# Attention backward on one core: dK/dV products of both key chunks in one step, and transposes in column tiles of 32

## The chip, the core and the metric

The kernel runs on one core of a Trainium2 chip. The core has a matrix engine (TensorE, PE in the profile; its weight loads are listed apart as PEld), a vector engine (VectorE, DVE), an activation engine (ScalarE, ACT), GpSimd (POOL) and SyncE (SP), which here issues most of the DMAs. The metric is the device time of one execution in microseconds (us). The kernel before took 2742.68 us, the median of 3 runs (2736.2 to 2745.76).

## What is computed

The reference takes the gradient of a block `x + attention(ln(x)) * silu(mlp(ln(ln(x))))` with respect to x and to all weights. Sequence length is 2048, model width 512, 32 heads of 16. What matters here is the attention with its backward pass. Cut to that part, the reference is

```
xn = layernorm(x);  qkv = xn @ wqkv
scores = einsum("bhqd,bhkd->bhqk", q, k) * (Dh ** -0.5)
p = softmax(scores);  o = einsum("bhqk,bhkd->bhqd", p, v);  s = o @ wo
out = x + s * g          # g = silu(mlp(xn))
# and jax.vjp of all this: d(x), d(wqkv), d(wo), d(w1), d(b1), d(w2), d(b2)
```

For each head the backward needs E = exp(scores), the products D = V dO^T, and G = E * D elementwise; then dQ from G K, and dK and dV from G^T Q, E^T Q and E^T dO, with the softmax's row sums folded into small weights.

## The kernel before

Three parts run one after the other: a part ahead (`phase_pre`: layer norms, projections, the MLP), the attention (`attention_core`), and the weight gradients (`phase3`). The change is in the attention alone. In the profile its first score product starts 285.7 us after the span's start and its last Z product ends at 2135.1 us, so it takes 1849 of the 2738 us.

**Blocks and steps.** Heads go in 16 pairs. For a pair, the 2048 queries are cut into 4 chunks of 512; pair and query chunk make a block, of which there are 64. A block goes over the 2048 keys in 16 key blocks of 128. One key block of one block is a *step* `g`: 1024 steps, `g % 16` is the place in the block. Four key blocks make a key chunk `kc`, and two key chunks a pair `kp`. The order of the instructions on each engine is written by hand: the loop at L841 emits, for each `g`, the calls at L853 to L869 in that order, and nothing reorders them (`manual_schedule`).

**What a step does.** On TensorE, in this order:

- `emit_z` (L786): Z products of an older block, 21 steps behind (`ZG`, `ZE`, L835). They are dK and dV for one key chunk and one quarter `qb` of the queries. Part 1 multiplies the transposed G (`Gk`) by the weights `W2`, part 0 the transposed E (`Ek`) by `W1`, each for two heads `hj`. An output is 32 rows of the accumulator Z at row `64*par + 32*hj`, `par = kc % 2`. `ZORD` (L605) alternates the even and the odd key chunk from step to step.
- `emit_s` and `emit_d` (L629, L647): s = K Q^T of the next step and d = V dO^T of this step, two heads each. Contraction is over 32 rows, and the four products sit in the four row groups of the array. Together they are called the score phase here.
- `emit_T` (L686, L694): in three steps of four (not where `g % 4 == 3`), the transpose of one quarter of the queries' E for the key chunk before: 8 transposes of 128x128 into one PSUM tile `tT`. The fourth quarter is transposed by a DMA (L678), and so is G (L674).
- `emit_x` (L707): X products of the step before, 6 of them with 32 (or 17) output rows each: `l` at rows 64 and 96, `e` at rows 0 and 32, `g` at rows 64 and 96.

ScalarE takes the exponentials of both s tiles (L635, `et`), and then copies `tT` to SBUF (L704, `ek`). VectorE multiplies d and E (L660, `gts`). Once per block, at step 2 (`FIN_AT`), TensorE transposes X (L744), and VectorE and GpSimd make from it the block's outputs and the weights W1 and W2 (`emit_fin`, L747). After every eight Z steps VectorE adds Z to `acc` (L821, steps 4 and 12).

**What sets who waits.** PSUM has three buffers for s and tT together (`ps_st`), three for d and the X transpose (`ps_d`), and one each for X and Z. A score product waits until ScalarE has read the buffer that it writes, a transpose group waits for the buffer of an earlier one, a d product waits for VectorE's multiply of an earlier d, and the first Z product of a key chunk pair waits until VectorE has read Z.

Of the kernel before, what the change touches and what calls it, by code (L numbers as in the profile page):

```python
# [9 lines left out]
f32 = mybir.dt.float32  # L10
# [532 lines left out]
def attention_core(ctx, tc, NAT_s, NATQ_s, Oall, dQall, dKVT_out, ident_f32, ident_bf, npairs=16, nqc=4):  # L543
    nc = tc.nc
# [5 lines left out]
    ps_z = ctx.enter_context(tc.tile_pool(name="ps_z", bufs=1, space=PSUM))  # L550
# [24 lines left out]
    acc = opnd.tile([128, 2, 512], f32, name="acc")  # L575

    def load_ops(p):
        t = OP[p % 2]

        def plain():  # L580
            nc.sync.dma_start(out=t["NAT"][:].rearrange("q k j c -> q k (j c)"), in_=NAT_s[p])
            nc.sync.dma_start(out=t["NATQq"][:].rearrange("q k j c -> q k (j c)"), in_=NATQ_s[0][p])
            nc.sync.dma_start(out=t["NATQd"][:].rearrange("q k j c -> q k (j c)"), in_=NATQ_s[1][p])

        def ck():
            nc.gpsimd.tensor_copy(out=Pad[:, :, 0:2, 0:17], in_=t["NAT"][:, :, :, 0:17])
            nc.gpsimd.tensor_copy(out=Pad[:, :, 2:4, 0:16], in_=t["NAT"][:, :, :, 17:33])

        def tk():
            nc.sync.dma_start_transpose(out=t["KVT"][:].rearrange("r (m k) -> r m k", m=16),  # L590
                                        in_=Pad[:].rearrange("q m j c -> q (m j c)"))

        def cq():
            nc.gpsimd.tensor_copy(out=Pad[:, :, 0:2, 0:17], in_=t["NATQq"][:])
            nc.gpsimd.tensor_copy(out=Pad[:, :, 2:4, 0:16], in_=t["NATQd"][:])

        def tq():
            nc.sync.dma_start_transpose(out=t["QDT"][:].rearrange("r (m k) -> r m k", m=16),
                                        in_=Pad[:].rearrange("q m j c -> q (m j c)"))
        return [plain, ck, tk, cq, tq]  # L600

    blocks = [(p, qc) for p in range(npairs) for qc in range(nqc)]
    NB = len(blocks)
    NSTEP = NB * 16
    ZORD = [((i // 8) * 2 + i % 2, (i % 8) // 2) for i in range(16)]  # L605
    st_s, st_d, st_et, st_gt, st_T = {}, {}, {}, {}, {}
    blk = [dict(Gk={}, Ek={}) for _ in range(NB)]
    cur = {}

    def a_unit(g):  # L610
        return (g // 16, g % 16) if 0 <= g < NSTEP else None

    def z_unit(g):
        j = g // 16
        return (j,) + ZORD[g % 16] if 0 <= j < NB else None

    def op_of(j):
        return OP[blocks[j][0] % 2]
# [1 line left out]
    def emit_s(g, hj):  # L620
        a = a_unit(g)
        if a is None:
            return
        j, kb = a
        op = op_of(j)
        qc = blocks[j][1]
        r = 32 * hj
        s = ps_st.tile([128, 512], f32, name="s", tag="st")
        nc.tensor.matmul(s[:], lhsT=op["KVT"][r:r + 32, kb * 128:(kb + 1) * 128], rhs=op["QDT"][r:r + 32, qc * 512:(qc + 1) * 512],  # L629
                         start=True, stop=True, tile_position=(r, 0))  # L630
        if hj == 0 and kb % 4 == 0:
            cur["et"] = etp.tile([128, 4, 4, 2, 128], bf16, name="et")
        et = cur["et"]
        st_et[g] = et
        nc.scalar.activation(out=et[:, :, kb % 4, hj, :], in_=s[:].rearrange("k (b q) -> k b q", b=4), func=ACT.Exp)  # L635

    def emit_d(g, hj):
        a = a_unit(g)
        if a is None:
            return  # L640
        j, kb = a
        op = op_of(j)
        qc = blocks[j][1]
        r = 64 + 32 * hj
        d = ps_d.tile([128, 512], f32, name="d", tag="d")
        st_d[g, hj] = d
        nc.tensor.matmul(d[:], lhsT=op["KVT"][r:r + 32, kb * 128:(kb + 1) * 128], rhs=op["QDT"][r:r + 32, qc * 512:(qc + 1) * 512],  # L647
                         start=True, stop=True, tile_position=(r, 0))
# [31 lines left out]
    def t_unit(g):  # L680
        a = a_unit(g - 4)
        if a is None or a[1] % 4 == 3:
            return None
        return a[0], a[1] // 4, a[1] % 4

    def emit_T(g):  # L686
        u = t_unit(g)
        if u is None:
            return
        j, kc, qb = u  # L690
        et = st_et[j * 16 + kc * 4 + 3]
        t = ps_st.tile([128, 8, 128], bf16, name="tT", tag="st")
        for b in range(8):
            nc.tensor.transpose(t[:, b, :], et[:, qb, b // 2, b % 2, :], ident_bf[:])  # L694
        st_T[g] = t

    def emit_cT(g):
# [30 lines left out]
    def emit_xs(g):  # L728
        a = a_unit(g)
        if a is None or a[1] != 15:  # L730
            return
        j = a[0]
        xs = xsp.tile([128, 512], f32, name="xs")
        nc.scalar.copy(out=xs[:], in_=blk[j].pop("X")[:])
        blk[j]["xs"] = xs

    def emit_XT(g):
        j = g // 16 - 1
        if g % 16 != FIN_AT or not 0 <= j < NB:
            return  # L740
        xs = blk[j].pop("xs")
        XT = ps_d.tile([128, 4, 128], f32, name="XT", tag="d")
        for qb in range(4):
            nc.tensor.transpose(XT[:, qb, :], xs[:, qb * 128:(qb + 1) * 128], ident_f32[:])  # L744
        blk[j]["XT"] = XT
# [37 lines left out]
        blk[j]["W1"] = W1  # L783
        blk[j]["W2"] = W2

    def emit_z(g, part):  # L786
        u = z_unit(g)
        if u is None:
            return
        j, kc, qb = u  # L790
        par = kc % 2
        if part == 1:
            if qb == 0 and par == 0:
                cur["Z"] = ps_z.tile([128, 512], f32, name="Z", tag="z")
                blk[j]["Z"] = cur["Z"]
            Z = cur["Z"]
            gv = blk[j]["Gk"][kc][:].rearrange("q a (r h b) k -> q a r h b k", r=2, h=2)
            for hj in range(2):
                r = 64 * par + 32 * hj
                nc.tensor.matmul(Z[r:r + 32, :], lhsT=blk[j]["W2"][:, qb, hj, :], rhs=gv[:, :, :, hj, qb, :],  # L800
                                 start=(qb == 0), stop=False, skip_group_check=True, tile_position=(0, r))
            return
        Z = blk[j]["Z"]
        ev = blk[j]["Ek"].pop((kc, qb))[:].rearrange("q (a h) k -> q h a k", h=2)
        for hj in range(2):
            r = 64 * par + 32 * hj
            nc.tensor.matmul(Z[r:r + 32, :], lhsT=blk[j]["W1"][:, qb, hj, :], rhs=ev[:, hj],  # L807
                             start=False, stop=(qb == 3), skip_group_check=True, tile_position=(0, r))

    def emit_acc(g):  # L810
        u = z_unit(g)
        if u is None or u[1] % 2 != 1 or u[2] != 3:
            return
        j, kc, qb = u
        p, qc = blocks[j]
        Z = blk[j]["Z"]
        av = acc[:, kc // 2, :]
        if qc == 0:
            nc.vector.tensor_copy(out=av, in_=Z[:])
        else:  # L820
            nc.vector.tensor_tensor(out=av, in0=Z[:], in1=av, op=ALU.add)  # L821
        if qc == nqc - 1:
            if kc == 1:
                cur["ob"] = outp.tile([128, 2, 512], bf16, name="ob")
            ob = cur["ob"]
            nc.gpsimd.tensor_copy(out=ob[:, kc // 2, :], in_=av)
            if kc == 3:
                def store():
                    dv = dKVT_out[p * 64:(p + 1) * 64, :].rearrange("r (a b s) -> r a b s", a=2, b=2)
                    for b in range(2):  # L830
                        nc.sync.dma_start(out=dv[:, :, b, :], in_=ob[b * 64:(b + 1) * 64])
                late.append((cur["g"] + 2, store))

    FIN_AT = 2
    ZG, ZE = -5, -5  # L835
    late = []
    for f in load_ops(0):
        f()
# [2 lines left out]
    for g in range(NSTEP + 16 + 8):  # L841
        cur["g"] = g
        a = a_unit(g)
        if a is not None:
            j, kb = a
            p, qc = blocks[j]
            if kb == 0 and qc == 1 and p + 1 < npairs:
                for i, f in enumerate(load_ops(p + 1)):
                    late.append((g + 1 + 4 * i, f))
        for it in [x for x in late if x[0] <= g]:  # L850
            late.remove(it)
            it[1]()
        emit_z(g + ZG - 16, 1)  # L853
        emit_z(g + ZE - 16, 0)
        emit_acc(g + ZE - 16)
        emit_s(g + 1, 0)
        emit_XT(g)
        emit_d(g, 0)
        emit_d(g, 1)
        emit_s(g + 1, 1)  # L860
        emit_mult(g)
        emit_fin(g)
        emit_T(g)
        emit_x(g - 1, "l")
        emit_x(g - 1, "e")
        emit_x(g - 1, "g")
        emit_xs(g - 1)
        emit_cT(g)
        emit_dmat(g)  # L869
        st_gt.pop(g - 2, None)  # L870
        st_et.pop(g - 12, None)
# [104 lines left out]
```

## Time and profile before

| | |
|---|---|
| median of 3 runs | 2742.68 us |
| profiled execution | 2740.01 us, its span 2738.2 us |
| granted TensorE clock, mean of the span | 0.956 |
| granted clock between 300 and 1900 us | 1.00 |
| attention, first s to last Z | 285.7 to 2135.1 us |
| PE / ACT / DVE busy, 700 to 1100 us | 384.4 / 332.5 / 315.1 of 400 us |
| instructions of PE and PEld | 24005 and 24064 |

A line of the timeline gives the start in us from the span's start, the time from the first start to the last end of a merged run of like instructions, the engine, the line of the kernel, the operation, what it writes and reads, the shapes, and how many instructions were merged. `128*32` ahead of the shapes is the part of the array that a matrix instruction uses, rows by columns. Matmuls are pipelined, so their starts tell more than their durations: a 128x512 product into a free part of the array shows 380 to 390 ns, but the next one on the same columns starts 215 ns after it. In a wait line the first name is the one who waited, the second the one that ended the wait, then come the total in us, how often, and the longest.

### The profile page before, as it was taken

How to read it: one execution, taken by the hardware profiler on the slowest of the kernel's cores; microseconds unless marked ns; L12 is line 12 of the kernel's file. 1: busy time of each engine (PE TensorE's matmuls, PEld its weight loads, DVE VectorE, ACT ScalarE, POOL GpSimd, SP SyncE). 2: the span in 40 equal slices, each digit the busy share in tenths (PEclk: the TensorE clock that was granted, in tenths of full speed). 3: DMA queues.
4: the chain of work that ended last, by engine and by line, in shares of the span. 5: the costliest groups of instructions: out<-in, count | busy, mean ns of one | idle time of the engine just before them, and what ended most of it. 6: DMA issues, size and time to landing. Idle time of an engine off the chain costs nothing. (4 is left out here: it accounts for less than half of the span.)

```text
span 2738.2 us, 61100 instructions
## 1 busy us (share of the span) xinstructions
PE 2372.0 (87%) x24005; PEld 1079.3 (39%) x24064; DVE 1910.5 (70%) x3190; ACT 1795.8 (66%) x3317; POOL 600.6 (22%) x990
## 2 busy tenths in 40 slices
PE   3687799999999999999999999999999666656967
PEld 2333344444444444444444444444444333332433
DVE  5755677787777787777778778777778458870144
ACT  3343788888888888888888878888888244430120
POOL 0434111011110110101111011110110338870034
PEclk8899899999999999999999999999999878887989
DMA  5334999999999999999999999999999643326331
GB/s 184 97 124 129 187 193 207 191 205 202 192 215 188 207 200 199 204 188 210 198 204 207 188 205 192 207 203 192 206 183 192 209 133 94 106 86 168 111 125 43
DMA packets 1564739, 477.08 MB, mean 174 GB/s; under 512 B 1484705, under 2 KB 1549602, under 8 KB 1564450
## 3 DMA queue, kind: packets, MB, share of 16 engines
q1 hardware_dynamic: 1491058, 419.56, 76.8%
q10 hardware_dynamic: 73392, 53.62, 6.4%
q8 instruction: 188, 3.08, 0.5%
q14 instruction: 101, 0.83, 0.1%
HBM read 65.41 MB, written 55.32 MB: 44 GB/s over the span
## 5 line engine op out<-in xcount | busy, mean ns | idle before, releaser
L660 DVE TENSOR_TENSOR gts<-d,et 128x512 bf16<-128x512 f32 x2048 | 1305.9, 685 | 399.1 <-PE s L629 179.1
L635 ACT ACTIVATE et<-s 128x512 bf16<-128x512 f32 x2048 | 1127.3, 597 | 305.8 <-PE s L629 211.7
L694 PE MATMUL tT<-ident_bf,et 128*128 128x128 bf16 x6144 | 475.1, 220 | 40.1 <-ACT ek L704 39.7
L629 PE MATMUL s<-QDT,KVT 32*128 32x512 bf16 x2048 | 478.2, 386 | 16.8 <-DMA QDT<-Pad 15.2
L647 PE MATMUL d<-QDT,KVT 32*128 32x512 bf16 x2048 | 443.1, 384 | 31.0 <-DVE gts L660 30.8
L704 ACT COPY ek<-tT 128x512 f32<-128x512 f32 x768 | 456.7, 595 | 0.8 <-PE tT L694 0.8
L694 PEld LDWEIGHTS <-et 128*128 128x128 bf16 x6144 | 353.8, 98 | 213.5 <-issue 199.2
L722 PE MATMUL X<-et,NAT 128*32 128x512 bf16 x2048 | 403.8, 391 | 0.0
L719 PE MATMUL X<-et,Lc 128*32 128x512 bf16 x2048 | 403.2, 390 | 0.0
L725 PE MATMUL X<-gts,NAT 128*17 128x512 bf16 x2048 | 393.1, 380 | 0.0
L800 PE MATMUL Z<-gk,W 128*32 128x512 bf16 x2048 | 390.6, 380 | 1.3 <-DVE acc L821 1.3
L807 PE MATMUL Z<-ek,W 128*32 128x512 bf16 x2048 | 390.4, 379 | 0.0
L629 PEld LDWEIGHTS <-KVT 32*128 32x128 bf16 x2048 | 126.2, 91 | 514.8 <-issue 509.0
L771 POOL TENSOR_TENSOR W<-NATQq,rL 128x128 bf16<-128x128 bf16 x64 | 25.5, 399 | 1223.6 <-DVE rL L766 1223.6
L719 PEld LDWEIGHTS <-Lc 128*32 128x32 bf16 x2048 | 98.2, 93 | 139.0 <-issue 59.5
L800 PEld LDWEIGHTS <-W 128*32 128x32 bf16 x2048 | 112.8, 96 | 87.7 <-issue 27.3
L807 PEld LDWEIGHTS <-W 128*32 128x32 bf16 x2048 | 103.6, 97 | 101.9 <-issue 0.3
L647 PEld LDWEIGHTS <-KVT 32*128 32x128 bf16 x2048 | 96.2, 91 | 11.4 <-issue 11.4
L722 PEld LDWEIGHTS <-NAT 128*32 128x32 bf16 x2048 | 98.5, 93 | 0.0
L421 PE MATMUL dh_tp<-ident_bf,dh 128*128 128x128 bf16 x224 | 30.1, 270 | 76.7 <-DVE dh L418 73.9
L725 PEld LDWEIGHTS <-NAT 128*17 128x17 bf16 x2048 | 95.3, 90 | 0.0
L448 PE MATMUL ps_dw<-dm_all,hgc 128*128 128x512 bf16 x220 | 54.8, 406 | 29.7 <-DMA hgc<-HG_s 29.4
(198 smaller groups left out, 2514.8 us busy)
## 6 DMA issues: line engine op xcount, KB each, us to landing
gk<-gts SPq DMA_TRANSPOSE x512, 4.1
HG_s<-hg SPq DMA_DIRECT2D x16, 448.0 KB, 2.6
DH_s<-dh ACTq DMA_DIRECT2D x16, 448.0 KB, 2.5
NAT<-NAT_s SPq DMA_DIRECT2D x16, 264.0 KB, 3.2
GB_s<-gB ACTq DMA_DIRECT2D x16, 256.0 KB, 2.0
ek<-et SPq DMA_TRANSPOSE x256, 3.2
dKVT_s<-ob SPq DMA_DIRECT2D x32, 128.0 KB, 2.5
dhc<-DH_s ACTq DMA_DIRECT2D x2, 2048.0 KB, 13.5
```

Of the source, the lines that this page charges most:

```text
L448: nc.tensor.matmul(ps[:], lhsT=hgc[:, t, :], rhs=dm_all[:, t, :], start=(t == 0), stop=(t == NT - 1))
L629: nc.tensor.matmul(s[:], lhsT=op["KVT"][r:r + 32, kb * 128:(kb + 1) * 128], rhs=op["QDT"][r:r + 32, qc * 512:(qc + 1) * 512], start=True, ...
L635: nc.scalar.activation(out=et[:, :, kb % 4, hj, :], in_=s[:].rearrange("k (b q) -> k b q", b=4), func=ACT.Exp)
L647: nc.tensor.matmul(d[:], lhsT=op["KVT"][r:r + 32, kb * 128:(kb + 1) * 128], rhs=op["QDT"][r:r + 32, qc * 512:(qc + 1) * 512], start=True, ...
L660: nc.vector.tensor_tensor(out=gts[:, kb % 2, hj, :].rearrange("k (b q) -> k b q", b=4), in0=st_d.pop((g, hj))[:].rearrange("k (b q) -> k b ...
L694: nc.tensor.transpose(t[:, b, :], et[:, qb, b // 2, b % 2, :], ident_bf[:])
L704: nc.scalar.copy(out=ek[:].rearrange("q a k -> q (a k)").bitcast(f32), in_=st_T.pop(g)[:].rearrange("q a k -> q (a k)").bitcast(f32))
L719: nc.tensor.matmul(X[64 + 32 * hj:96 + 32 * hj, :], lhsT=Lc[:], rhs=et[:, :, kb % 4, hj, :], start=(kb == 0), stop=False, skip_group_check ...
L722: nc.tensor.matmul(X[32 * hj:32 * hj + 32, :], lhsT=NATt[:, kb, hj, 1:33], rhs=et[:, :, kb % 4, hj, :], start=(kb == 0), stop=(kb == 15), ...
L725: nc.tensor.matmul(X[64 + 32 * hj:64 + 32 * hj + 17, :], lhsT=NATt[:, kb, hj, 0:17], rhs=st_gt[g][:, kb % 2, hj, :], start=False, stop=(kb ...
L800: nc.tensor.matmul(Z[r:r + 32, :], lhsT=blk[j]["W2"][:, qb, hj, :], rhs=gv[:, :, :, hj, qb, :], start=(qb == 0), stop=False, skip_group_ch ...
L807: nc.tensor.matmul(Z[r:r + 32, :], lhsT=blk[j]["W1"][:, qb, hj, :], rhs=ev[:, hj], start=False, stop=(qb == 3), skip_group_check=True, til ...
```

## The change

Two things change, both in the instructions that TensorE gets.

1. Z products. Before, a step did G and E parts of one key chunk (4 products: G at two row positions, then E at the same two). Now a step does one part for both key chunks of the pair: all four G products (rows 0, 32, 64, 96) in one step, all four E products in the next. Number and size of the products stay the same, and so does the distance of 21 steps.
2. Transposes of E. Before, one transpose took 128x128 at once (one weight load of 128 columns and one matmul with 128 moving columns). Now it is cut into four, each with 32 columns of E as weights, placed in the column group that its output rows belong to. A group of 8 becomes 32 weight loads and 32 matmuls, each matmul with 128 moving columns as before.

```diff
-    ZORD = [((i // 8) * 2 + i % 2, (i % 8) // 2) for i in range(16)]
...
     def z_unit(g):
         j = g // 16
-        return (j,) + ZORD[g % 16] if 0 <= j < NB else None
+        m = (g % 16) // 2
+        return (j, m // 4, m % 4, g % 2) if 0 <= j < NB else None
...
         for b in range(8):
-            nc.tensor.transpose(t[:, b, :], et[:, qb, b // 2, b % 2, :], ident_bf[:])
+            for c in range(0, 128, 32):
+                nc.tensor.transpose(t[c:c + 32, b, :], et[:, qb, b // 2, b % 2, c:c + 32], ident_bf[:], tile_position=(0, c))
...
-    def emit_z(g, part):
+    def emit_z(g):
         u = z_unit(g)
         if u is None:
             return
-        j, kc, qb = u
-        par = kc % 2
-        if part == 1:
-            if qb == 0 and par == 0:
-                cur["Z"] = ps_z.tile([128, 512], f32, name="Z", tag="z")
-                blk[j]["Z"] = cur["Z"]
-            Z = cur["Z"]
-            gv = blk[j]["Gk"][kc][:].rearrange("q a (r h b) k -> q a r h b k", r=2, h=2)
+        j, kp, qb, part = u
+        if part == 0 and qb == 0:
+            blk[j]["Z"] = ps_z.tile([128, 512], f32, name="Z", tag="z")
+        Z = blk[j]["Z"]
+        for par in range(2):
+            kc = 2 * kp + par
+            if part == 0:
+                W = blk[j]["W2"]
+                mv = blk[j]["Gk"][kc][:].rearrange("q a (r h b) k -> q h b a r k", r=2, h=2)[:, :, qb]
+            else:
+                W = blk[j]["W1"]
+                mv = blk[j]["Ek"].pop((kc, qb))[:].rearrange("q (a h) k -> q h a k", h=2)
             for hj in range(2):
                 r = 64 * par + 32 * hj
-                nc.tensor.matmul(Z[r:r + 32, :], lhsT=blk[j]["W2"][:, qb, hj, :], rhs=gv[:, :, :, hj, qb, :],
-                                 start=(qb == 0), stop=False, skip_group_check=True, tile_position=(0, r))
-            return
-        Z = blk[j]["Z"]
-        ev = blk[j]["Ek"].pop((kc, qb))[:].rearrange("q (a h) k -> q h a k", h=2)
-        for hj in range(2):
-            r = 64 * par + 32 * hj
-            nc.tensor.matmul(Z[r:r + 32, :], lhsT=blk[j]["W1"][:, qb, hj, :], rhs=ev[:, hj],
-                             start=False, stop=(qb == 3), skip_group_check=True, tile_position=(0, r))
+                nc.tensor.matmul(Z[r:r + 32, :], lhsT=W[:, qb, hj, :], rhs=mv[:, hj],
+                                 start=(part == 0 and qb == 0), stop=(part == 1 and qb == 3), skip_group_check=True,
+                                 tile_position=(0, r))
...
-    ZG, ZE = -5, -5
+    ZOFF = -21
...
-        emit_z(g + ZG - 16, 1)
-        emit_z(g + ZE - 16, 0)
-        emit_acc(g + ZE - 16)
+        emit_z(g + ZOFF)
+        emit_acc(g + ZOFF)
```

`emit_acc` follows the new numbering; it still runs after every eighth Z step, at steps 4 and 12.

More of the change, by code (lines that the diff above doesn't have):

```diff
@@ L789, in emit_z @@
             return
-        j, kc, qb = u
-        par = kc % 2
-        if part == 1:
-            if qb == 0 and par == 0:
-                cur["Z"] = ps_z.tile([128, 512], f32, name="Z", tag="z")
-                blk[j]["Z"] = cur["Z"]
-            Z = cur["Z"]
-            gv = blk[j]["Gk"][kc][:].rearrange("q a (r h b) k -> q a r h b k", r=2, h=2)
+        j, kp, qb, part = u
[10 more added lines that the diff above has]
+                mv = blk[j]["Ek"].pop((kc, qb))[:].rearrange("q (a h) k -> q h a k", h=2)
             for hj in range(2):
                 r = 64 * par + 32 * hj
-                nc.tensor.matmul(Z[r:r + 32, :], lhsT=blk[j]["W2"][:, qb, hj, :], rhs=gv[:, :, :, hj, qb, :],
-                                 start=(qb == 0), stop=False, skip_group_check=True, tile_position=(0, r))
-            return
-        Z = blk[j]["Z"]
-        ev = blk[j]["Ek"].pop((kc, qb))[:].rearrange("q (a h) k -> q h a k", h=2)
-        for hj in range(2):
-            r = 64 * par + 32 * hj
-            nc.tensor.matmul(Z[r:r + 32, :], lhsT=blk[j]["W1"][:, qb, hj, :], rhs=ev[:, hj],
-                             start=False, stop=(qb == 3), skip_group_check=True, tile_position=(0, r))
+                nc.tensor.matmul(Z[r:r + 32, :], lhsT=W[:, qb, hj, :], rhs=mv[:, hj],
+                                 start=(part == 0 and qb == 0), stop=(part == 1 and qb == 3), skip_group_check=True,
+                                 tile_position=(0, r))
     def emit_acc(g):
         u = z_unit(g)
-        if u is None or u[1] % 2 != 1 or u[2] != 3:
+        if u is None or u[2] != 3 or u[3] != 1:
             return
-        j, kc, qb = u
+        j, kp = u[0], u[1]
         p, qc = blocks[j]
         Z = blk[j]["Z"]
-        av = acc[:, kc // 2, :]
+        av = acc[:, kp, :]
         if qc == 0:
@@ L822, in emit_acc @@
         if qc == nqc - 1:
-            if kc == 1:
+            if kp == 0:
                 cur["ob"] = outp.tile([128, 2, 512], bf16, name="ob")
             ob = cur["ob"]
-            nc.gpsimd.tensor_copy(out=ob[:, kc // 2, :], in_=av)
-            if kc == 3:
+            nc.gpsimd.tensor_copy(out=ob[:, kp, :], in_=av)
+            if kp == 1:
                 def store():
```

## The prediction

> **What bounds the kernel now.** I read the page first, then the waits, then the timeline of one block (1203.24 to 1231.78 us). Page and waits:
>
> ```profile
> PE 2372.0 (87%) x24005; PEld 1079.3 (39%) x24064; DVE 1910.5 (70%) x3190; ACT 1795.8 (66%) x3317; POOL 600.6 (22%) x990
> ```
> ```profile
> 700.00:1100.00 400.00, 384.39 (x4510) 169.52 (x4504) 315.08 (x530) 332.52 (x627) 53.12 (x143) 1.00 1.04 199
> ```
> ```profile
> PE tT L694 <- ACT ek L704: 39.7, 62, 0.8
> ```
>
> The second is the windows view: PE 384 of 400 us, ACT 332, DVE 315, clock 1.00. TensorE is never idle for long in the attention, but the other two follow at 83% and 79%, so a shorter TensorE step can only be spent until one of them is late. The one wait of note on TensorE is a transpose group on ScalarE's copy.
>
> The timeline of steps 8 and 9 shows what a step is made of:
>
> ```profile
> 1218.74 0.39 PE L629 MATMUL s<-QDT,KVT 32*128 32x512 bf16 x1
> ...
> 1219.07 0.62 PE L694 MATMUL tT<-ident_bf,et 128*128 128x128 bf16 x8
> ...
> 1219.62 0.40 PE L719 MATMUL X<-et,Lc 128*32 128x512 bf16 x2
> ...
> 1219.62 0.39 PE L722 MATMUL X<-et,NAT 128*32 128x512 bf16 x2
> ...
> 1219.84 0.38 PE L725 MATMUL X<-gts,NAT 128*17 128x512 bf16 x2
> 1219.85 0.38 PE L800 MATMUL Z<-gk,W 128*32 128x512 bf16 x2
> ...
> 1220.07 0.38 PE L807 MATMUL Z<-ek,W 128*32 128x512 bf16 x2
> 1220.13 0.59 ACT L704 COPY ek<-tT 128x512 f32<-128x512 f32 x1
> ...
> 1220.38 0.38 PE L629 MATMUL s<-QDT,KVT 32*128 32x512 bf16 x1
> ...
> 1220.78 0.61 PE L694 MATMUL tT<-ident_bf,et 128*128 128x128 bf16 x8
> 1220.80 1.09 ACT L635 ACTIVATE et<-s 128x512 bf16<-128x512 f32 x2
> ...
> 1221.54 0.38 PE L725 MATMUL X<-gts,NAT 128*17 128x512 bf16 x2
> ...
> 1221.76 0.38 PE L800 MATMUL Z<-gk,W 128*32 128x512 bf16 x2
> ```
>
> Three things to see. Products in different column groups start together (19.62, four X products), and the next on the same columns 0.22 later. In step 8's tail Z's G part fits beside X's g part (19.84 and 19.85, other columns), in step 9's it needs the columns that g holds and comes 0.22 later (21.54, 21.76): odd and even key chunks take turns, so every other step has four slots of 0.215 us instead of three. And whenever the array's shape changes, about 0.1 us is lost: 8 transposes at 0.056 (two groups of four in 0.22, see the last fence) are 0.45, yet 19.07 to 19.62 is 0.55; the last Z slot (20.07) and the next s (20.38) are 0.31 apart instead of 0.215.
>
> The score phases start at 1218.74, 1220.38, 1222.29, 1223.93 and 1225.23: steps of 1.64, 1.91, 1.64, 1.30, or 6.49 us for four. The whole block takes 28.54: places 0 to 2 4.19, 2 to 5 6.47, 5 to 8 4.84, 8 to 12 6.49, 12 to 16 6.55. 64 blocks are 1827 of the attention's 1849 us.
>
> **The change on TensorE alone.** Z: all four column groups in one step, so the tail is always three slots: X's l and e; X's g beside Z's rows 0 and 32; Z's rows 64 and 96. Eight of 16 steps lose 0.215. Transposes: the same 8 x 0.056 = 0.45 if four column groups run side by side, and X then uses the same shape (128*32), so the 0.10 behind the group goes, in 12 of 16 steps. Together 1.72 + 1.20 = 2.92 us per block, 187 us in all. Nothing else moves: DMAs, their order on SP, the POOL work, and the number of waits by kind on each engine are as before.
>
> **What a cut transpose costs** is not in the trace. Below: 0.45 a group, since 128 moving columns per column group stay (0.056 each). Above: if none of the 32 overlapped, 32 x 0.056 = 1.79. The nearest rows:
>
> ```profile
> 285.72 0.13 PEld L629 LDWEIGHTS <-KVT 32*128 32x128 bf16 x3 [16.11 <-issue]
> 285.75 0.61 PE L629 MATMUL s<-QDT,KVT 32*128 32x512 bf16 x2 [15.23 <-DMA QDT<-Pad]
> 285.76 0.10 PEld L647 LDWEIGHTS <-KVT 32*128 32x128 bf16 x2
> 285.76 0.60 PE L647 MATMUL d<-QDT,KVT 32*128 32x512 bf16 x2
> 285.76 0.11 PEld L629 LDWEIGHTS <-KVT 32*128 32x128 bf16 x1
> ...
> 2208.51 0.38 PE L367 MATMUL w_tp<-ident_bf,w_sb 128*128 128x128 bf16 x4
> 2208.73 0.38 PE L416 MATMUL ps_dhg<-w2T,dmT 128*128 128x512 bf16 x1
> ```
>
> At 285.72 TensorE comes out of a 16 us wait and starts ten loads and matmuls within 0.05 us, 5 ns each; 64 at that rate are 0.32, less than 0.45. The four X products at 19.62 show four column groups streaming together. I take 0.45. At 2208.73 a product follows four transposes of its own array shape after 0.22 = 4 x 0.056: the gap behind a group belongs to the shape, not to transposing, so it should go.
>
> A page of the Trainium skill speaks against the cut. "TensorE: Matmul & The Clock Gate", Part 1 ("Wait — 56ns, not 53.3ns?"), says that starts of matmuls are never less than about 25 ns apart, however small. By it a group would take an estimated 32 x 25 ns = 0.80 us and the time would be about 2815. The X products at 19.62 start closer together than that, so I go by the rows.
>
> **What the other engines leave of it.** A group needs the buffer that the previous group's copy frees, and that copy stands behind two exponentials. From a score phase to the first exponential 0.42 (20.38 to 20.80), two spacings of 0.49 and 0.48, the copy 0.59, the signal 0.05: the next group cannot start before 2.035 after that score phase. The trace shows it: 1218.74 + 2.035 = 1220.775, and the group starts at 1220.78 instead of 0.33 after 1220.38. Step 9's slack hides it today; steps of 0.33 + 0.45 + 0.765 = 1.54 do not. Likewise d waits for VectorE: the first multiply of a step ends 1.27 after its score phase, and the step without transposes shrinks to 1.30 - 0.215 = 1.085.
>
> Four steps from a score phase at 0: group at 0.51 (0.185 waiting for d, 0.325 to the group); score phase 0.51 + 1.215 = 1.725; group at the later of 2.05 and 2.035; score 3.265; group at the later of 3.59 and 1.725 + 2.035 = 3.76; score 4.975; no group, score 6.06. So 6.06 against 6.49, not 5.71 (3 x 1.54 + 1.085).
>
> By places. 0 to 2: ScalarE's extra copy of X holds the second group until about 2.745, as now (2.68), then 1.215: 3.96. 2 to 5: from score phase to the group of step 4 it is VectorE's chain (multiplies, X copy, the small operations, multiply: 5.055 from 1207.43 to 1212.48), and Z then waits for `acc` until 5.93; Z's single slot follows, 0.215 + 0.095: 6.24, which is 0.23 less. 5 to 8: d waits 0.285 for the multiply behind `acc`, groups at 0.605 and 2.145, last step 1.085: 4.445. 8 to 12: 6.06. 12 to 16: the same and 0.07 that `acc` adds through d: 6.13. Sum 26.84, or 1.70 less a block, 109 us.
>
> The profiled execution took 2740.0 (span 2738.2; the median of the three runs is 2.7 higher). 2740.0 - 109 = 2631, so **2630**.
>
> Costed at nothing: the G transposes by DMA must land before their buffer comes round again, six steps later. They land 4.1 us after issue, `gts` waits for one 13 times (14.3 us in all); six steps shrink from some 10.7 to 10.1 us. Without that cover 0.1 for each of 512 would be 51 us. TensorE's instructions go from 47,700 to 84,500; they are fetched in 188 pieces of 16 KB, hidden today. About 145 more at 1 us unhidden would be 145 us; one piece would be used in 5 to 6 us, so I count none.
>
> **Rivals.** (1) TensorE alone sets the pace, because the waits give way in some order I do not see: the full 187, 2553. Against it stands the wait at 1220.78. (2) The gap behind the group stays, or the group takes 0.55: each group step is 0.10 longer, part of it inside the waits; the same sums give 6.26 for four steps and 27.5 a block, 2675. Against it: the product at 2208.73. (3) The cut transposes run at their own pace of more than 0.056 per four. With a group at 0.65 to 0.68 us (21 ns a pair) four steps take 6.49 again and the gain is gone; at 0.80 four steps take 6.94 and the block 1.2 more, 2817; at 1.79 some 13 us more, 3590. For it: loads and matmuls at such density appear nowhere in this trace over more than ten instructions. Against it: those ten. That is the rival on the other side. (4) The cut is merged or reordered into no change: against it, TensorE's instruction list has 32 pairs a group.
>
> **How the numbers follow.** Forecast 0.58, rival 1 0.15, rival 2 0.12, rival 3 0.12, no difference 0.03. One measurement of this kernel tells 0.3%, about 8 us, from no change. Faster: 0.58 + 0.15 + 0.12 = 0.85; same 0.03; slower 0.12. The range runs from 2555 (rival 1) to 2720 (rival 2 with a group of 0.60 to 0.65); the slow rival is left out above. The forecast's own range is 2595 to 2660.
>
> **What will show it.** Transposes 32 to a group, 0.45 from the first to the first X product, and no gap of 0.1 there: right; 0.8: rival 3. X's g and half of Z together in every step, the other half 0.22 later: the three slots. Waits "tT on ek" of some 0.15 to 0.2 us in two of four steps, hundreds instead of 62, and "d on gts" in hundreds instead of 73: the forecast; if both stay rare and the block comes to 25.7, rival 1. PE's share of 400 us should fall from 384 to about 370. Wrong would be the forecast if Z or X waited on a DMA, or if PE sat idle with "issue" in front of the transposes.

## The result, and the profile after

The changed kernel takes 2766.1 us (median of 4) against 2743.0 us for the kernel before, measured beside it: ratio 1.009, 95% interval 1.0067 to 1.0112. The forecast was 2630. It is slower, by 23 us, where it was to be 113 us faster.

The page of after, with the busy line, TensorE's and the DMA transposes' queues (share of 16 engines' span last), the group of `gts` and the issues:

```profile
PE 2293.6 (83%) x42437; PEld 1065.0 (39%) x42496; DVE 1895.9 (69%) x3190; ACT 1804.8 (65%) x3317; POOL 600.8 (22%) x990
...
q1 hardware_dynamic: 1491058, 419.56, 87.0%
...
q8 instruction: 332, 5.44, 0.8%
...
L660 DVE TENSOR_TENSOR gts<-d,et 128x512 bf16<-128x512 f32 x2048 | 1288.2, 683 | 442.5 <-DMA gk<-gts 172.8
...
gk<-gts SPq DMA_TRANSPOSE x512, 5.4
...
ek<-et SPq DMA_TRANSPOSE x256, 4.2
```

The same lines of before that the prediction did not show:

```profile
q1 hardware_dynamic: 1491058, 419.56, 76.8%
...
q8 instruction: 188, 3.08, 0.5%
...
gk<-gts SPq DMA_TRANSPOSE x512, 4.1
...
ek<-et SPq DMA_TRANSPOSE x256, 3.2
```

TensorE is busy 78 us less, as it should be, but in a longer span. Queue 1 moves the same packets and bytes and takes 10 points more of the engines' time for them. Queue 8 brings TensorE's instructions: 332 pieces of 16 KB instead of 188, and 144 pieces for the cut's 36,864 more instructions make 256 to a piece. A G transpose lands 5.4 us after its issue instead of 4.1, an E transpose 4.2 instead of 3.2.

The stretch of the windows view that was shown of before (PE, PEld, DVE, ACT, POOL, then clock, DMA share, GB/s), and the waits that matter (total, times, longest):

```profile
700.00:1100.00 400.00, 366.08 (x8496) 165.82 (x8488) 310.28 (x528) 332.74 (x625) 53.48 (x144) 0.98 1.21 200
```
```profile
DVE gts L660 <- DMA gk<-gts: 172.8, 108, 5.3
...
PE d L647 <- DVE gts L660: 135.4, 163, 4.3
...
PE tT L695 <- ACT ek L705: 29.1, 53, 0.9
```

TensorE's 366 us are 18 less than before, yet no more steps are done: VectorE's work in the stretch falls from 315 to 310. The wait of `gts` for its G transposes went from 14.3 to 172.8 us, and TensorE's d products wait behind it, now up to 4.3 us at a time.

The timeline of two undisturbed steps:

```profile
1202.46 0.63 PE L695 MATMUL tT<-ident_bf,et 128*32 128x128 bf16 x32
1202.91 0.38 PE L723 MATMUL X<-et,NAT 128*32 128x512 bf16 x2
...
1203.13 0.38 PE L805 MATMUL Z<-ek,W 128*32 128x512 bf16 x2
1203.14 0.38 PE L726 MATMUL X<-gts,NAT 128*17 128x512 bf16 x2
1203.35 0.38 PE L805 MATMUL Z<-ek,W 128*32 128x512 bf16 x2
1203.67 0.39 PE L629 MATMUL s<-QDT,KVT 32*128 32x512 bf16 x1
...
1203.99 0.63 PE L695 MATMUL tT<-ident_bf,et 128*32 128x128 bf16 x32
1204.45 0.38 PE L723 MATMUL X<-et,NAT 128*32 128x512 bf16 x2
```

This is the step as forecast: 32 transposes in 0.45 to 0.46 us, no gap behind them, three slots in odd and even steps alike. And here is one of the long stalls, first SyncE's queue, then VectorE, then TensorE (each a timeline of its own):

```profile
804.11 1.26 SPq L678 DMA_TRANSPOSE ek<-et  x1
805.46 3.17 SPq L590 DMA_TRANSPOSE KVT<-Pad  x1
808.73 5.32 SPq L674 DMA_TRANSPOSE gk<-gts  x2
814.13 1.26 SPq L678 DMA_TRANSPOSE ek<-et  x1
```
```profile
806.87 2.48 DVE L660 TENSOR_TENSOR gts<-d,et 128x512 bf16<-128x512 f32 x4
814.63 2.48 DVE L660 TENSOR_TENSOR gts<-d,et 128x512 bf16<-128x512 f32 x4 [5.29 <-DMA gk<-gts]
```
```profile
815.38 0.37 PE L647 MATMUL d<-QDT,KVT 32*128 32x512 bf16 x1 [4.32 <-DVE gts L660]
...
817.60 1.04 PE L695 MATMUL tT<-ident_bf,et 128*32 128x128 bf16 x32
818.43 0.64 PE L723 MATMUL X<-et,NAT 128*32 128x512 bf16 x2
```

SyncE's queue has no pause. `gts` has three buffers, the transposes that read them are issued late (here behind one of `ek` and one of `KVT`) and slowly, so VectorE stands for 5.29 us and TensorE for 4.32. After the pause TensorE runs slower for some 4 us: the same 32 transposes take 0.83 (817.60 to 818.43). The windows view gives a clock of 0.66 from 815 to 820.

Where the time went, by the steps: I take the distance from one step's d products to the next, by place in the block, over all 64 blocks: the sum of the 16 medians is the pace of an undisturbed block, the mean of the blocks is what was really spent. Before: 28.54 and 28.74 us. After: 27.24 and 29.21 (the last place has a stall in more than half of the blocks; without that it is 26.83, see the runs with four buffers or without E's DMA transposes below). So the pace fell by the forecast 1.7 us, and stalls grew from 0.2 to 2.4 us a block.

### The profile page after: what moved, and what is told of

Read it like the earlier page. It is cut to its first block, busy times and chain, and to the rows that moved or that the text cites. A ratio compares the mean times of both kernels' runs of the same rounds, so it can differ in the third digit from the quotient of the medians.

```text
span 2762.0 us, 97964 instructions
## 1 busy us (share of the span) xinstructions
PE 2293.6 (83%) x42437; PEld 1065.0 (39%) x42496; DVE 1895.9 (69%) x3190; ACT 1804.8 (65%) x3317; POOL 600.8 (22%) x990
## 3 DMA queue, kind: packets, MB, share of 16 engines
q8 instruction: 332, 5.44, 0.8%
## 5 line engine op out<-in xcount | busy, mean ns | idle before, releaser
L660 DVE TENSOR_TENSOR gts<-d,et 128x512 bf16<-128x512 f32 x2048 | 1288.2, 683 | 442.5 <-DMA gk<-gts 172.8
L647 PE MATMUL d<-QDT,KVT 32*128 32x512 bf16 x2048 | 537.8, 387 | 136.6 <-DVE gts L660 135.4
L629 PE MATMUL s<-QDT,KVT 32*128 32x512 bf16 x2048 | 576.4, 390 | 16.9 <-DMA QDT<-Pad 15.3
L695 PE MATMUL tT<-ident_bf,et 128*32 128x128 bf16 x24576 | 492.1, 222 | 34.8 <-ACT ek L705 29.1
L695 PEld LDWEIGHTS <-et 128*32 128x32 bf16 x24576 | 368.0, 97 | 211.4 <-issue 193.8
L629 PEld LDWEIGHTS <-KVT 32*128 32x128 bf16 x2048 | 151.1, 91 | 669.7 <-issue 658.4
L805 PE MATMUL Z<-ek,W 128*32 128x512 bf16 x2048 | 310.8, 386 | 0.0
L805 PE MATMUL Z<-gk,W 128*32 128x512 bf16 x2048 | 288.4, 385 | 1.3 <-DVE acc L820 1.3
L805 PEld LDWEIGHTS <-W 128*32 128x32 bf16 x4096 | 199.4, 97 | 153.8 <-issue 59.9
L647 PEld LDWEIGHTS <-KVT 32*128 32x128 bf16 x2048 | 96.6, 91 | 13.3 <-issue 13.1
L427 PE MATMUL ps_dy<-w1T,dh1T 128*128 128x512 bf16 x208 | 66.7, 464 | 3.6 <-ACT dh1T L422 3.4
```

The lines of the kernel that those rows point to most:

```text
L427: nc.tensor.matmul(ps[:], lhsT=dh1T[:, fc, :], rhs=w1T[:, fc, :], start=(fc == 0), stop=(fc == FC - 1))
L660: nc.vector.tensor_tensor(out=gts[:, kb % 2, hj, :].rearrange("k (b q) -> k b q", b=4), in0=st_d.pop((g, hj))[:].rearrange("k (b q) -> k b ...
L695: nc.tensor.transpose(t[c:c + 32, b, :], et[:, qb, b // 2, b % 2, c:c + 32], ident_bf[:], tile_position=(0, c))
L805: nc.tensor.matmul(Z[r:r + 32, :], lhsT=W[:, qb, hj, :], rhs=mv[:, hj], start=(part == 0 and qb == 0), stop=(part == 1 and qb == 3), skip_ ...
```

## The experiments

Theory B, formed from the trace of after: the cut makes TensorE's instruction stream 1.8 times as long; each 16 KB fetch (1.0 to 1.1 us) holds up the DMA transposes that run at that moment; SyncE's queue, which issues them one after the other, is then full and `gts` waits. The trace speaks for it: from 300 to 2100 us, packets of queue 1 that last 1000 ns or more number 2515 before and 5376 after, 99% of them overlap a fetch in both, and there are 16 to 18 for each fetch (158 before, 295 after). The issue of a G transpose takes 3.00 us on average when a fetch falls into it (248 of 492 in after) and 1.9 when none does. Before it is 2.80 (126 of 501) and 1.76. Theory A, in the first four expectations: the queue sets the pace by itself once the steps are short. In those four, B leaves open whether the fetches or the cut transposes slow the DMAs; theory C, added later, says that it is the narrow tiles, by what they read or write, and not the number of instructions. A last rival needs no theory: the cut transposes or the new Z order could cost TensorE more than their pace says.

All runs in one table. Fetches and packets of 1 us and more are counted from the DMA records of 300 to 2100 us; "SyncE" is the time in which its queue was issuing (semaphore instructions, about 1 point of the share, included), per block (its share of those 1800 us times the mean block); pace and mean block as above. `after_noek` and `z_noek` leave a part of the computation out.

| kernel | us | ratio to before [95%] | fetches | long packets | G lands, us | SyncE, us a block | pace | mean block |
|---|---|---|---|---|---|---|---|---|
| before | 2740.5 | | 158 | 2515 | 4.1 | 23.6 (82%) | 28.54 | 28.74 |
| z_only | 2691.5 | 0.9835 [0.980, 0.987] | 162 | 2597 | 4.2 | 23.7 (85%) | 27.59 | 27.98 |
| z_gtp4 | 2667.0 | 0.9732 [0.972, 0.975] | 162 | 2632 | 4.2 | 23.5 (85%) | 27.59 | 27.58 |
| pad6 | 2725.0 | 0.9953 [0.994, 0.997] | 205 | 3615 | 4.8 | 24.9 (87%) | 27.59 | 28.63 |
| z_cut64 | 2732.5 | 0.9964 [0.995, 0.998] | 206 | 3699 | 4.8 | 25.1 (88%) | 27.74 | 28.59 |
| after | 2766.1 | 1.009 [1.007, 1.011] | 295 | 5376 | 5.4 | 27.4 (94%) | 27.24 | 29.21 |
| pad18 | 2779.5 | 1.0145 [1.013, 1.016] | 291 | 5340 | 5.2 | 27.0 (92%) | 27.79 | 29.35 |
| t_only | 2786.4 | 1.0166 [1.014, 1.019] | 291 | 5325 | 5.4 | 27.3 (92%) | 27.93 | 29.55 |
| after_gtp4 | 2743.6 | 1.0011 [1.000, 1.002] | 299 | 5791 | 5.5 | 27.7 (96%) | 26.83 | 28.78 |
| after_noek | 2649.4 | 0.9668 [0.965, 0.969] | 307 | 4041 | 4.8 | 19.9 (73%) | 26.83 | 27.33 |
| z_noek | 2667.5 | 0.9736 [0.972, 0.975] | 163 | 1766 | 3.9 | 16.9 (61%) | 27.59 | 27.63 |
| z_shift | 2811.3 | 1.0264 [1.025, 1.028] | 152 | 2775 | 4.9 | 28.2 (94%) | 27.92 | 29.89 |
| z_pad6 | 2834.0 | 1.0349 [1.033, 1.037] | 194 | 3665 | 5.2 | 28.8 (95%) | 28.25 | 30.25 |
| z_pad | 2909.9 | 1.0623 [1.061, 1.064] | 272 | 4869 | 5.6 | 29.8 (95%) | 29.32 | 31.28 |
| z_ms | 2984.7 | 1.0894 [1.088, 1.091] | 141 | 2263 | 4.8 | 27.7 (86%) | 31.26 | 32.27 |

**Each part alone.** `z_only` keeps the new order of Z and takes the cut away:

```diff
         for b in range(8):
-            for c in range(0, 128, 32):
-                nc.tensor.transpose(t[c:c + 32, b, :], et[:, qb, b // 2, b % 2, c:c + 32], ident_bf[:], tile_position=(0, c))
+            nc.tensor.transpose(t[:, b, :], et[:, qb, b // 2, b % 2, :], ident_bf[:])
```

> The new order of the Z products alone; the transposes stay 128 wide, so TensorE has as many instructions as before. Theory A (the G and E transposes that SyncE issues set the pace once the compute steps are short; SyncE was occupied 82% of the attention before and 94% after): compute alone would allow about 2675, but SyncE reaches some 90%, gts waits for gk 60 to 120 us instead of 14, time 2700 to 2760. Theory B (the cut transposes, or their doubled instruction fetch, slow the DMAs): gk lands after 4.1 us as before, gts waits for gk under 30 us, time 2660 to 2690.

`t_only` is the kernel before with the cut alone (the same edit the other way round).

> The cut transposes alone, with the old order of the Z products. Compute alone would allow about 2690. Theory A: SyncE some 88 to 92% occupied, waits of gts for gk between those of the two kernels, time 2690 to 2750. Theory B: gk lands after 5.4 us as in the changed kernel, whatever the pace, and the time is 2750 or more.

2691.5 and 2786.4 us. On TensorE both parts gain (pace 27.59 and 27.93 against 28.54, so 0.95 and 0.61 us a block), and the results lie on different sides of before. The new Z order keeps most of its 0.95 us (mean block 0.76 less). It lies between the ranges of A and B, in time and in the wait of `gts` (38.4 us, 14.3 before): a little of A is there without any more fetches. `t_only` is as B expected, with landing 5.4 us and 27.3 us of SyncE a block, as in after. That rules out the Z order as the cause of the loss, and leaves B or C for the cut.

**Relief for SyncE's queue.** `after_noek` has the cut, but no DMA transposes of E:

```diff
-        if kb % 4 == 3:
-            ek = ekp.tile([128, 8, 128], bf16, name="ek")
-            blk[j]["Ek"][(kc, 3)] = ek
-            nc.sync.dma_start_transpose(out=ek[:], in_=st_et[g][:, 3].rearrange("k a h q -> k (a h q)"))
...
+        if qb == 2:
+            blk[j]["Ek"][(kc, 3)] = ek
```

> The changed kernel without the 256 DMA transposes of E: the fourth quarter's E products read the third quarter's transposed tile, so dK and dV of that quarter are not computed. Compute is the same, SyncE loses about 350 us of its 1690. Theory A: gts waits for gk under 30 us, a block goes to the 26.8 us that compute allows, time 2625 to 2660. Theory B: the G transposes stay slow (5 us or more to landing) and the time stays above 2700.

`z_noek` is the same edit on `z_only`.

> The new order of the E products, uncut transposes, and no DMA transposes of E: the products of the fourth quarter read the third quarter's transposed tile, so that part of dK is left out. The same omission with the cut gave 2649.4 us. The step times say that the cut is worth 27.59 - 26.83 = 0.76 us a block, 49 us over 64 blocks, where the DMA transposes keep up: if that gain is real, this run is 2670 to 2695 us, slower than with the cut. If the cut gains nothing even there, it is 2650 us or less.

2649.4 with the cut and 2667.5 without. The time of `after_noek` is what A expected, and B's "stays above 2700" was wrong: fetches do most of their harm where the queue has no room for them. Where SyncE's queue is at 73%, the cut does gain, 18 us (`z_noek` is 2.5 us under the range expected). That is less than the 49 us that the pace offers: `after_noek` still spends 0.5 us a block beyond its pace, and `gts` waits 44.6 us for G transposes that land in 4.8 instead of 3.9 us. The fetches cost something even here.

**One buffer more.** `after_gtp4` gives `gts` four buffers. The room comes from one `ek` buffer fewer, which the E part going first in each pair of steps allows:

```diff
-    gtp = sb("gtp", 3)
+    gtp = sb("gtp", 4)
...
-    ekp = sb("ekp", 19)
+    ekp = sb("ekp", 18)
...
-        return (j, m // 4, m % 4, g % 2) if 0 <= j < NB else None
+        return (j, m // 4, m % 4, 1 - g % 2) if 0 <= j < NB else None
...
```

The lines left out let `Z`, its `start` and `stop` and `emit_acc` follow the new order.

> The changed kernel with four gts buffers instead of three; to make room the E part of a quarter goes ahead of its G part, which needs 18 ek buffers instead of 19. If the transposes are only late now and then (latency), two more steps of room take most of the waits away: 2640 to 2680. If SyncE's queue is full on average (throughput), it goes from 94% to 97 or more and the time falls by no more than 60, to 2705 to 2750.

`z_gtp4` is the same on `z_only` (one `ek` buffer fewer here too, not two).

> The new order of the E products, uncut transposes, and four buffers for the tile that the DMA transposes of G read instead of three (two fewer for E's). VectorE waits for those transposes 38.4 us in the version with three buffers. If those waits lie on the path, 2665 to 2685 us; if TensorE's own pace sets the time there, 2691 us as with three. With the cut the same edit brought 2766 to 2744 us.

With the cut the buffer brings 22.5 us and no more: SyncE's queue goes to 96%, and a deeper buffer does not make a full queue faster (the second of the two cases expected). Without the cut it brings 24.5 us, the waits of `gts` for G transposes vanish from the list, and the mean block equals the pace. 2667.0 us is the best of these kernels that do the whole computation, 2.7% under before (0.9717 to 0.9746). It is the change's first part with a fourth buffer.

**Instructions without the cut.** The first two attempts, `z_pad` and `z_pad6`, add tiny products of zeros to `z_only` in each third slot, where their column groups are idle, with a new tile of zeros (`z_pad`; in `z_pad6` it is `range(6)`):

```diff
+    Zc = opnd.tile([128, 32], bf16, name="Zc")
+    nc.gpsimd.memset(Zc[:], 0.0)
...
+        for n in range(18):
+            r = 32 * (n % 2)
+            nc.tensor.matmul(Z[r:r + 32, 0:1], lhsT=Zc[:], rhs=Zc[:, 0:1], start=False, stop=(part == 1 and qb == 3),
+                             skip_group_check=True, tile_position=(0, r))
```

> The kernel with the new order of the E products and uncut transposes (2691.5 us), plus 36,864 tiny products of zeros on TensorE (lhsT a zero tile of 32 columns, one moving column, 18 in each third slot), which is as many instructions as the cut adds. Nothing is read or transposed in narrower tiles. Theory B (each 16 KB fetch of TensorE's instructions holds up a DMA transpose): fetches in 300 to 2100 us rise from 162 to about 295, packets of 1000 ns and more from 2597 to about 5300, the median G transpose issue to about 2.4 us, SyncE's queue to 92% or more, and the time to 2760 us or above. Theory C (it is the narrow tiles, by what they read from SBUF or write to PSUM, that disturb the DMAs): G transposes land in 4.2 us as before, SyncE's queue stays near 85%, and the time is 2690 to 2710 us.

> The new order of the E products, uncut transposes, and 6 tiny products of zeros in each third slot where the run with 18 took 2909.9 us: 12,288 instructions more on TensorE, as many as the cut into 64 columns adds (2732.5 us). Theory B: about 206 fetches in 300 to 2100 us, some 3700 packets of 1000 ns and more, SyncE's queue near 88%, and 2720 to 2750 us. If what hurt with 18 was the kind of the tiny products and not their count, the fetches rise alike and the time stays at 2691 to 2705 us; if the kind adds to the count, it is above 2750 us.

2909.9 and 2834.0 us, both far above what B expected for their number of instructions (2834 against z_cut64's 2732.5 for the same 12,288). The records showed why they do not count as a test: packets of 256 bytes on queue 1 (those of the DMA transposes) that last 30 to 100 ns had gone from some 8,300 to 80,000 and 100,000 in 300 to 2100 us. The new tile of 64 bytes a partition had moved every tile behind it, those of the DMA transposes among them, by the tiles' sizes from addresses that divide by 256 (the kernel has the tile `pad_to_256b` ahead of them) to addresses 64 past that. `z_shift` has the tile and none of the products:

```diff
+    Zc = opnd.tile([128, 32], bf16, name="Zc")
+    nc.gpsimd.memset(Zc[:], 0.0)
```

> The new order of the E products, uncut transposes, no instruction added but one memset; a tile of 64 bytes a partition is put ahead of the tiles that the DMA transposes read and write, which then begin 64 bytes later. If that is what the run with 6 tiny products paid beyond the cut into 64 columns (2834 against 2732 us): some 100,000 packets of 30 to 100 ns where there were 8,300, G transposes landing in 4.7 us or more, 2750 to 2800 us. If the place of the tiles does not matter: 2691 us.

2811.3 us, over the range expected: the move alone costs 120 us, with 110,353 such packets of 30 to 100 ns and only 152 fetches. `pad18` and `pad6` have the products and not the move. They multiply the existing tile `Lc`, whose column 0 is zero (`pad18`; in `pad6` it is `range(6)`):

```diff
+        for n in range(18):
+            r = 32 * (n % 2)
+            nc.tensor.matmul(Z[r:r + 32, 0:1], lhsT=Lc[:], rhs=Lc[:, 0:1], start=False, stop=(part == 1 and qb == 3),
+                             skip_group_check=True, tile_position=(0, r))
```

> The new order of the E products, uncut transposes, 18 tiny products of zeros in each third slot as in the run of 2909.9 us, but taken from an existing tile, so that no new tile of 64 bytes moves the tiles behind it. 36,864 instructions more on TensorE, as many as the cut adds. Theory B: about 295 fetches in 300 to 2100 us, 5300 long packets, G transposes landing in 5.4 us, SyncE's queue at 92 to 96%, 2760 to 2810 us, near the cut kernel's own 2766. If the fetches are harmless and the moved tiles were what cost 218 us: 2691 to 2710 us.

> The same with 6 tiny products, 12,288 instructions more, as the cut into 64 columns. Theory B: 206 fetches, 3700 long packets, SyncE's queue near 88%, 2715 to 2740 us (the cut into 64 columns took 2732.5). If the fetches are harmless: 2691 us.

2779.5 and 2725.0 us. The tile's view of `gk` (first line: issue time in ns, least, median, most; then who waited, in us and times; then landing), of z_only and of pad18:

```profile
L674 SPq DMA_TRANSPOSE gk<-gts x512: 1316/1793/3849, 288.8 to 2074.8; - x171
...
  DVE gts L660: 41.8, 30
...
DMA to landing us min/median/max: 3.7/4.2/6.9
```
```profile
L674 SPq DMA_TRANSPOSE gk<-gts x512: 1317/2298/4387, 290.4 to 2162.3; - x171
...
  DVE gts L660: 130.3, 80
...
DMA to landing us min/median/max: 3.7/5.2/6.5
```

and the lines of after that answer to them (this view books a few waits of `gts` more than the list of waits):

```profile
L674 SPq DMA_TRANSPOSE gk<-gts x512: 1317/2386/5063, 289.6 to 2153.4; - x171
...
  DVE gts L660: 189.4, 121
...
DMA to landing us min/median/max: 3.8/5.4/7.4
```

The transposes of pad18 are uncut, its added products do no work, and with 6 of them the pace of the steps does not move at all (27.59, places 1.635 and 1.082 us as in z_only). Yet its fetches, long packets and landing times are near those of the cut kernels, and so are its waits and time (130.3 us and 2779.5 us; `t_only` 132.8 and 2786.4, after 189.4 and 2766.1). That is what B says and C denies: the number of TensorE's instructions is enough, whatever they do. That it acts by the fetches, and not by what the tiny products read, shows in the G transposes' issues: with no fetch in it one takes 1.86 us on average in pad18 and 1.80 in z_only, with a fetch 2.96 and 2.82. What grew is the share that meets a fetch, from 127 of 508 to 244 of 490.

**The dose.** `z_cut64` cuts into two tiles of 64 columns:

```diff
-            nc.tensor.transpose(t[:, b, :], et[:, qb, b // 2, b % 2, :], ident_bf[:])
+            for c in range(0, 128, 64):
+                nc.tensor.transpose(t[c:c + 64, b, :], et[:, qb, b // 2, b % 2, c:c + 64], ident_bf[:], tile_position=(0, c))
```

> The new order of the E products, with each transpose of E cut into two tiles of 64 columns instead of four of 32: 12,288 instructions more than without a cut, a third of what the full cut adds. Theory B: fetches in 300 to 2100 us about 210 (162 uncut, 295 with four), packets of 1000 ns and more about 3500, SyncE's queue near 88%, and a time between the two, 2700 to 2725 us. Theory C: narrow tiles in full number, so G transposes land in 5 us or more and the time is 2750 us or above; if neither count nor tiles matter, 2691 us.

2732.5 us, 41 above `z_only` and 7.5 above B's range, with 206 fetches; `pad6`, with the same count and no cut, is 33.4 above. With `z_only` that makes three points near one line: 48 more pieces over the run cost `pad6` 33.4 us, 144 more cost `pad18` 88, or 0.6 to 0.7 us a piece. With 64 columns the array's shape still changes at X (a group at 1204.02, its X at 1204.59, so 0.57 us as before), and the pace is no better than uncut (27.74 against 27.59), so `z_cut64` has the cost and none of the gain.

**On another engine.** `z_ms` puts the 12,288 instructions on GpSimd:

```diff
+    Zc = opnd.tile([128, 32], bf16, name="Zc")
...
+        for n in range(12):
+            nc.gpsimd.memset(Zc[0:1, 0:1], 0.0)
```

> The new order of the E products, uncut transposes, TensorE's instructions untouched, and 12 one-element memsets on the otherwise idle GpSimd in each third slot: 12,288 instructions more, on another engine. Theory B (a fetch of any engine's instructions goes through the same DMA engines): fetches as in the two kernels with 12,288 more on TensorE, about 206, SyncE's queue near 88%, G transposes landing in 4.8 us, and 2720 to 2750 us. If only TensorE's fetches do harm, or GpSimd's are taken another way: 2691 us as without them.

2984.7 us, and inconclusive: it has the moved tiles too, and the memsets (92 ns each) made GpSimd, which was not idle but busy for 22% of the span without them, late with the weights, so that TensorE's first Z product of a block waited:

```profile
PE Z L805 <- POOL W L772: 156.4, 60, 8.3
```

One thing can be read from it all the same. GpSimd's instructions came by queue 14 in pieces of 8 KB (198 where there were 101), each about 0.31 us. The packets of 1 us and more did not rise (2263), but pieces this short could hardly stretch a packet to 1 us: a G transpose's issue that met such a piece and none of TensorE's took 2.61 us on average (88 of them), and 2.15 when it met neither (306). A longer issue also meets more pieces, so this points to harm from GpSimd's fetches too and does not show it; what they cost was not tried further.

## Why the prediction was wrong

The step that failed is the last "costed at nothing": TensorE's instructions "are fetched in 188 pieces of 16 KB, hidden today. About 145 more at 1 us unhidden would be 145 us; one piece would be used in 5 to 6 us, so I count none." I asked whether TensorE would run out of instructions, and it does not. I did not ask what else passes through the DMA engines while a piece is fetched. After took 144 pieces more (48,069 and 84,933 instructions by the pages), and lies 135 us above the forecast for TensorE's pace (2766 - 2631).

Not all of that is the pieces' doing. The Z order alone, without one more fetch, gained 0.95 us a block in pace, or 61 us, and ran 12 us behind that (2691.5 where 2679.7 was due). This belongs to the other term put at nothing, the cover of the G transposes: a fourth buffer takes the waits away (2667.0). The other 123 us came when the cut was added (75 us lost where its pace gains 48): 0.85 us a piece. That this is near the price that was written down and set aside is luck, for that price was meant for TensorE waiting for its instructions. At the slower paces of `pad18` and `t_only` a piece costs 0.6 us (88 us over `z_only`; 85 us over what the pace of 27.93 allows). A likely reason for the difference, argued and not shown by a run of its own, is that the faster pace leaves SyncE's queue less room: 27.4 us of issuing a block do not fit into 26.84, while 27.0 and 27.3 just fit into 27.79 and 27.93.

The rest, point by point:

- **Cut transposes at 0.45 us a group**: right (1202.46 to 1202.91). So rival 3 did not happen, although the time moved the way that it alone had forecast. The page of the Trainium skill weighed there ("TensorE: Matmul & The Clock Gate", Part 1) sets about 25 ns between starts of matmuls. That sentence does not speak of matmuls in different column groups; here 32 in 0.45 us are 14 ns apart on average (by the records, four start 3 to 4 ns apart, one in each column group, and the next four 56 ns later). For that case the measurement decides against the rule.
- **The gap of 0.1 us behind the group goes**: right, and with 128x32 only (`z_cut64` keeps it); rival 2 is out.
- **Three slots in every step**: right (1203.13 to 1203.35; the step without transposes takes 1.082 us, forecast 1.085).
- **The block's sum of 26.84**: right as a pace, place by place. In `after_noek`, by medians from score phase to score phase, places 0 to 2 take 3.98 (forecast 3.96), 2 to 5 6.26 (6.24), 5 to 8 4.41 (4.445), 8 to 12 6.05 (6.06), 12 to 16 6.13 (6.13), in all 26.83. The chains of ScalarE and VectorE that were to keep TensorE from the full gain are there, so rival 1 is out as well. What was to show them in the list of waits was misjudged: "tT on ek" is booked 53 times in after, not hundreds. Steps of 1.72 and 1.71 us beside 1.54 show the two delays; the list does not.
- **"Nothing else moves: DMAs, their order on SP"**: the order is the same and the durations are not. The cover named for the G transposes (landing in 4.1 us before their buffer comes round) was right as a risk; its bound of 51 us was too small, since landing went to 5.4 and `gts` waited 172.8 us.
- **What would make it wrong**: "if Z or X waited on a DMA, or if PE sat idle with 'issue'". The wait on a DMA came, one engine further back, at VectorE.

The Trainium skill's "Runtime: NRT & Kernel Launch", "Instruction fetch mechanics", describes fetches in 16 KiB blocks by a DMA queue of the engine's own and calls the cost of a block "mostly hidden". The size agrees (5.44 MB in 332 pieces). Hidden it is for TensorE, and not for the DMA transposes beside it: 33.4 us for 48 pieces, 88 us for 144.

How a fetch holds up a transpose (which engine, ring or memory the two share) is not settled. Shown are the overlap, the dose, that the count alone is enough, and that issues which meet no fetch stay nearly as long as they were (1.80 and 1.86 us).

## What to carry to other kernels

Count instructions as DMA traffic: an edit that splits matrix work into more instructions added one 16 KB fetch for each 256 here, and as another stage lives by DMA transposes on one nearly full issuing queue, each fetch cost 0.6 to 0.85 us of the kernel's time. Before speeding up the busiest engine, write down how full the next queue is (here SyncE's, 82%, which the page's busy line does not list) and what it must deliver per step of the new pace. Split a two-part change: here one part alone, with one more buffer, was 2.7% faster, and the other part took it all away.

## What the runs showed of the hardware

- Sixty-four bytes matter. Tiles of the DMA transposes that begin 64 bytes past a multiple of 256 cost 120 us (`z_shift` against `z_only`): the median packet stays at 18 ns, but 110,353 of those of 256 bytes take 30 to 100 ns where 8,321 did. A page of the Trainium skill ("DMA: Bandwidth & Descriptors", "How a descriptor splits into AXI transactions") says that a transfer that doesn't start at a multiple of 256 bytes starts reading at the multiple below, and that the unused bytes "still cost beats", which agrees in kind. Whether the source or the destination tile is the one that pays was not tried. An experiment that adds a tile changes addresses, and that can be larger than the effect it is after (`z_pad6` against `pad6`: 109 us).
- A pause has a tail. After 4.32 us of idling at 811 to 815 us, TensorE's clock was 0.66 over the next 5 us and its group took 0.83 us instead of 0.45. Over 300 to 2000 us the granted clock was 0.98 in after and 1.00 in before, by estimate at most some 34 us (2% of 1700). That it follows the stalls and not the cut shows in `z_shift`, which has uncut transposes and 0.97, and in `after_noek`, which has the cut, few stalls and 1.00.
- TensorE takes weight loads of 32 columns, each with its matmul, in four column groups at 14 ns a pair on average: four of them in the 0.056 us that one transpose with 128 columns of weights needed before.
